# Gathered rows of five experts and of the last piece turned by transposing transfers instead of TensorE

## The chip, the cores and the metric

The kernel runs on one core of a Trainium2 chip, in one launch. The metric is the device time of an execution in microseconds (us); lower is better. The engines named below are TensorE (in rows PE, and PEld for its loads of stationary operands), VectorE (DVE), ScalarE (ACT), GpSimd (POOL) and SyncE (SP), whose queue issues most transfers.

## The reference

```python
# attention: an RWKV-5 recurrence over S = 768 steps, B = 4, H = 8, D = 48
for t in range(S):
    kt, vt, rt = k[:, :, t], v[:, :, t], r[:, :, t]
    cur = einsum('bhd,bhe->bhde', u * kt, vt)
    y[:, :, t] = einsum('bhd,bhde->bhe', rt, state + cur)
    state = w * state + einsum('bhd,bhe->bhde', kt, vt)
x = y.transpose(0, 2, 1, 3).reshape(3072, 384)
# balanced mixture of experts: 8 experts, each takes 384 tokens, by falling logit
logits = x @ w_gate
order = argsort(-logits.flatten())      # greedy: a token to its first expert with room
for e in range(8):
    mask = assigned == e
    out[mask] = relu(x[mask] @ w1[e]) @ w2[e]      # w1: 384 x 1024, w2: 1024 x 384
```

All numbers are 32-bit floats.

## The kernel before

The first 150 us or so compute the attention, the logits and the first pieces of the greedy assignment. From then on the experts run one after another, in the order in which the search on VectorE finds their tokens; expert number n below is the n-th in that order, and a last piece of 128 tokens (number 8) ends the work.

For each expert `fetch` gathers three pieces of 128 token rows of 384 floats out of DRAM into `xg` (indirect transfers on GpSimd's queue, L1518) and loads 3 MB of weights on SP's queue (L1511). The weights, `xg` and the turned rows `xT` lie in one of two pools, `self.turns[n % 2]`. The first layer contracts over the 384 features, so the rows have to be turned: `turned` (L1533) transposes each piece in three blocks of 128x128 on TensorE into a PSUM tile of `ps_t` (two buffers), and ScalarE copies each piece to `xT` (L1534).

The hidden layer is computed either directly (`hidden`, L1624; its first matmul reads all 384 rows of `xT`) or, for experts 3, 6 and 7, by a scheme of seven products (`hidden_by_seven`, L1601) that needs sums of blocks of `xT` made on VectorE (`row_sums`, L1559). The second layer: experts 1 to 5 compute two thirds of their output by seven products (`seven`, L1698) and the third piece directly (`result`, L1756). Experts 6 and 7 use fifteen products (`fifteen`, `products`, L1729).

In `seven` the products go in the order P1, P2, P5, P6, P3, P7, P4. P1, P6, P7 and P4 accumulate in one bank A, P5 and P3 in a bank B; what stands in A after P1, P6 and P7 is copied by ScalarE (L1703) before the next product adds to it, and VectorE adds the sums (L1688). Both banks are the two buffers of `ps_o`, from which `result` takes its own bank. The turn of the next expert's rows is called between P7 and P4:

```python
if name == "P4":
    between()
```

For experts 6 and 7 the turn of the next rows is called from `progress`, when the last of its due times, 1.75 (three quarters through the fifteen products), has passed. There each group of four products has a bank of `ps_o`, which ScalarE copies when the group is done (L1733).

The instructions of an engine run in the order in which they were issued. That order is chosen when the program is built: a planner takes what it holds to be ready, earlier lines of the program first, so the order can differ from the program's. `tc.issue_after(i)` keeps what is issued under it behind instruction i on that engine. The search for later experts' tokens is a chain of small VectorE instructions and a few small matmuls, spread among the products by `progress`.

Of the kernel before, what the change touches and what calls it, by code (L numbers as in the profile page):

```python
# [10 lines left out]
F32 = mybir.dt.float32  # L11
BF16 = mybir.dt.bfloat16
F16 = mybir.dt.float16
I32 = mybir.dt.int32
U8 = mybir.dt.uint8
AF = mybir.ActivationFunctionType
ALU = mybir.AluOpType
AX = mybir.AxisListType
# [1434 lines left out]
def rwkv5_eagle_then_base_layer_balanced(  # L1453
# [12 lines left out]
    nc = tc.nc  # L1466
    N, DX = out.shape
    E, _, F = moe_w1.shape
    NT = N // 128
    CAP = N // E  # L1470
# [17 lines left out]
    class Experts:  # L1488

        def __init__(self):  # L1490
            self.turns = []

        def open(self, ctx, i, **how):
            self.turns.append(ctx.enter_context(tc.tile_pool(name=f"f_turn{i}", bufs=1, **how)))

        def open_rest(self, ctx, **how):
            pool = lambda name, bufs, **kw: ctx.enter_context(tc.tile_pool(name=name, bufs=bufs, **kw))
            self.h, self.o, self.sums = pool("f_h", 2, **how), pool("f_o", 2, **how), pool("f_sums", 1, **how)
            self.first = pool("f_first", 1, **how)
            self.ps_t, self.ps_h, self.ps_o = (pool(f"f_ps_{x}", 2, space=PSUM, **how) for x in "tho")  # L1500

        def load_weights(self, n, fmax):
# [34 lines left out]
        def turn(self, ahead):  # L1537
            *_, xT = self.turned(ahead, lambda c: self.ps_t.tile([128, KD, 128], F32, name="xT_ps"))
            return xT

        def weight_sums(self, w1):
            H = F // 2
# [137 lines left out]
        def seven(self, left, right, tok, rows, at_product, between):  # L1680
            D = DX // 2
            o_sb = self.o.tile([128, NC, DX], F32, name="o_all")
            B = self.ps_o.tile([128, D], F32, name="pb_ps", tag="o_ps")
            A = self.ps_o.tile([128, D], F32, name="pa_ps", tag="o_ps")
            kept = {}

            def added(i, k, name, ps):
                nc.vector.tensor_tensor(out=o_sb[:, i, ts(k, D)], in0=kept[name], in1=ps, op=ADD)  # L1688

            for step, (name, a, b) in enumerate(self.SEVEN):  # L1690
                if name == "P2":
                    ps = self.ps_t.tile([128, D], F32, name="pc_ps", tag="xT_ps")
                else:
                    ps = B if name in ("P5", "P3") else A
                if name == "P4":
                    between()
                for j in range(KF // 2):
                    nc.tensor.matmul(ps, left[a][:, j, :], right[b][:, j, :],  # L1698
                                     start=(j == 0 and name in ("P1", "P2", "P5")), stop=(j == KF // 2 - 1),
                                     skip_group_check=True)  # L1700
                if name in ("P1", "P5", "P6", "P7"):
                    kept[name] = self.sums.tile([128, D], F32, name=f"kept_{name}")
                    nc.scalar.copy(kept[name], ps)  # L1703
                if name == "P2":
                    added(0, 0, "P1", ps)
                elif name == "P3":
                    added(0, 1, "P6", ps)
                elif name == "P7":
                    added(1, 1, "P5", kept["P7"])
                elif name == "P4":  # L1710
                    nc.scalar.copy(o_sb[:, 1, 0:D], ps)
                at_product((step + 1) / len(self.SEVEN))
            for c in range(2):
                self.leave(o_sb[:, c, :], tok[:, c:c + 1], next(rows))

        def products(self, products, out_sums, left, right, tok, rows, at_product, nk, ni):
            D = DX // nk
            count = sum(len(group) for group in products)
            own = sum(name[0] not in "po" for group in out_sums for name, _, _, _ in group)
            res = self.sums.tile([128, count + own, D], F32, name=f"res{count}")  # L1720
            o_sb = self.o.tile([128, NC, DX], F32, name="o_all")
            at = {f"o{i * nk + k}": o_sb[:, i, ts(k, D)] for i in range(ni) for k in range(nk)}
            n = 0
            for group, after in zip(products, out_sums):
                m = len(group)
                ps = self.ps_o.tile([128, m, D], F32, name="p_ps", tag="o_ps")
                for q, (name, a, b) in enumerate(group):
                    for j in range(KF // 2):
                        nc.tensor.matmul(ps[:, q, :], left[a][:, j, :], right[b][:, j, :],  # L1729
                                         start=(j == 0), stop=(j == KF // 2 - 1))  # L1730
                    at[name] = res[:, n + q, :]
                    at_product((n + q + 1) / count)
                nc.scalar.copy(res[:, n:n + m, :], ps)  # L1733
                n += m
                for name, a, op, b in after:
                    if name not in at:
                        at[name] = res[:, count + sum(k[0] not in "po" for k in at), :]
                    nc.vector.tensor_tensor(out=at[name], in0=at[a], in1=at[b], op=op)  # L1738
            for c in range(ni):
                self.leave(o_sb[:, c, :], tok[:, c:c + 1], next(rows))  # L1740
# [22 lines left out]
            self.scatter(o_sb, tok[:, c:c + 1], to)  # L1763

        FIRST_BY_SEVEN = 3, 6, 7

        def run(self, ahead, later, rows, pulls={}, xT=None):
            xT, lead = xT or self.turn(ahead), True
            row_sums = weight_sums = None
            while ahead:  # L1770
                n, _, tok, w1, w2 = ahead
                nb = tok.shape[1]
                whole = nb == NC
                many = whole and n in (E - 2, E - 1)
                sums = dict(row_sums or {}, **weight_sums) if weight_sums else None
                row_sums = weight_sums = None
                ahead = next((a for a in later if a), None)
                after = ahead and ahead[0] in self.FIRST_BY_SEVEN and ahead[2].shape[1] == NC
                late, lead = lead and not many, False
                right = (self.fifteen_w2 if many else self.seven_w2)(w2) if whole and not late else None  # L1780
                left = {}
                some = pulls.get(n, 2)
                due = [1.55, 1.75] if some == 2 else [0.75 + 1.15 * i / (some - 1) for i in range(some)]

                def half(hid):
                    nonlocal right
                    for name, (i, j) in self.BLOCKS.items():
                        left[name] = hid[:, ts(j, KF // 2), ts(i, 128)]
                    if many:
                        return  # L1790
                    last = self.sums_of(left, self.SEVEN_EARLY)
                    if late:
                        with tc.issue_after(last.ins):
                            right = self.seven_w2(w2)

                def turn():
                    nonlocal xT, row_sums
                    if ahead:
                        xT = self.turn(ahead)
                        if after:  # L1800
                            row_sums = self.row_sums(xT)

                def progress(t):
                    nonlocal weight_sums
                    if after and t > 1.1 and not weight_sums:
                        weight_sums = self.weight_sums(ahead[3])
                    while due and t > due[0]:
                        due.pop(0)
                        next(later, None)
                        if many and not due:  # L1810
                            turn()

                def at_product(part):
                    progress(1 + part)

                if sums:
                    hid = self.hidden_by_seven(sums, sums, progress)
                    half(hid)
                else:
                    hid = self.hidden(w1, xT, nb * 128, half if whole else lambda hid: None, progress, late)  # L1820
                if many:
                    self.sums_of(left, self.HID_SUMS)
                    self.fifteen(left, right, tok, rows, at_product)
                    continue
                if whole:
                    self.sums_of(left, self.SEVEN_LATE)
                    self.seven(left, right, tok, rows, at_product, turn)
                for c in range(NC - 1 if whole else 0, nb):
                    if c == nb - 1 and not whole:
                        turn()  # L1830
                    self.result(c, hid, w2, tok, next(rows))

# [186 lines left out]
```

## Time and profile before

| what | value |
|---|---|
| median of 3 runs | 394.67 us (394.22 to 394.68) |
| the profiled execution, its time | 393.36 us |
| its span | 391.6 us |
| mean granted TensorE clock, as a share of full speed | 0.995 |
| TensorE matmuls busy | 377.2 us, 96% |
| VectorE, ScalarE, GpSimd busy | 281.4, 169.3, 141.2 us |

The span runs from the first to the last instruction of one profiled execution; what lies around it is start and end. Times in rows are us from the span's start. Matmuls are pipelined, so the loads (PEld) show better than the matmuls when TensorE starts something new.

### The profile page before, as it was taken

Reading aid. Unit: us, or ns where it says so; the run is one execution under the profiler, and the core shown is the slowest. Engines: PE = TensorE matmul, PEld = TensorE weight load, DVE = VectorE, ACT = ScalarE, POOL = GpSimd, SP = SyncE. Lnnn points to the kernel's source line nnn. Section 1 sums busy time; section 2 is a strip of 40 time slices with the busy share of each in tenths; the row PEclk is TensorE's granted clock in tenths of the full one; section 3 lists DMA queues with packets and bytes.
Section 4 is the critical chain, followed back from the end, with each engine's and each line's share of the span. In section 5 each row is a group of like instructions: output and inputs, shape, how many; then the busy total and the mean of one; then the engine's idle time right before and its main releaser. Section 6 shows DMA issues by size and latency. Waiting matters only on the chain. (4 is left out here: it accounts for less than half of the span.)

```text
span 391.6 us, 9858 instructions
## 1 busy us (share of the span) xinstructions
PE 377.2 (96%) x3777; PEld 306.2 (78%) x3777; DVE 281.4 (72%) x959; ACT 169.3 (43%) x452; POOL 141.2 (36%) x173
## 2 busy tenths in 40 slices
PE   8899999999999999999999999999999999999992
PEld 7677888888877866687578899558657889989991
DVE  6755777586885788985949949888378976994530
ACT  4997989888883311312222242121222234234220
POOL 7878887767732022032122021203203212070020
PEclk9999999999999999999999999999999999999997
DMA  9999999988692164651560560109209264280010
GB/s 121 160 180 174 210 189 201 174 171 157 129 338 82 43 241 181 195 190 42 164 238 28 168 251 20 41 5 345 77 20 338 85 231 173 52 329 24 2 62 27
DMA packets 95335, 57.35 MB, mean 146 GB/s; under 512 B 77232, under 2 KB 89520, under 8 KB 95280
## 3 DMA queue, kind: packets, MB, share of 16 engines
q1 hardware_dynamic: 91936, 47.21, 48.0%
q0 software_dynamic: 3104, 9.44, 7.0%
q8 instruction: 31, 0.51, 0.6%
q14 instruction: 24, 0.20, 0.2%
q10 hardware_dynamic: 240, 0.00, 0.0%
HBM read 47.20 MB, written 9.44 MB: 145 GB/s over the span
## 5 line engine op out<-in xcount | busy, mean ns | idle before, releaser
L1624 PE MATMUL h_ps<-xT,w 128*128 128x384 f32 (+1 forms) x264 | 72.6, 427 | 0.0
L495 ACT ACTIVATE AT<-ident,dd 128x128 f32<-128x128 f32 x192 | 59.6, 392 | 2.2 <-DVE dd L448 2.1
L1624 PEld LDWEIGHTS h_ps<-xT,w 128*128 128x128 f32 x264 | 42.0, 191 | 19.6 <-issue 2.2
L1518 POOL DMA_INDIRECT xg<-x_rows,tok x22 | 22.5, 1021 | 92.4 <-PE h_ps L1624 23.7
L1750 POOL DMA_INDIRECT out_dram<-o_all,to x16 | 20.8, 1299 | 85.3 <-DVE o_all L1738 22.2
L1627 ACT ACTIVATE hid<-h_ps 128x384 f32<-128x384 f32 (+1 forms) x40 | 17.9, 449 | 54.2 <-PE h_ps L1624 50.9
L512 DVE COPY_PREDICATED AT<-mask,g_ps 64x512 f32<-64x512 uint8 (+1 forms) x48 | 32.4, 723 | 11.7 <-PE g_ps L505 9.9
L1756 PE MATMUL o_ps<-w,hid 128*128 128x384 f32 x96 | 32.5, 490 | 0.0
L505 PE MATMUL g_ps<-rT,kT 48*64 48x128 f32 (+1 forms) x768 | 26.3, 255 | 1.8 <-DVE AT L512 1.0
L436 POOL TENSOR_TENSOR kss<-krs,wk 128x384 f32<-128x384 f32 x24 | 24.3, 1016 | 8.0 <-DVE krs L340 5.0
L1756 PEld LDWEIGHTS o_ps<-w,hid 128*128 128x128 f32 x96 | 17.7, 190 | 10.6 <-issue 0.5
L545 PE MATMUL y_ps<-AT,vts 128*64 128x128 f32 x384 | 25.7, 276 | 0.0
L443 POOL TENSOR_TENSOR rk<-rk,u_bc 128x384 f32<-128x384 f32 x24 | 24.1, 1003 | 1.9
L505 PEld LDWEIGHTS g_ps<-rT,kT 48*64 48x64 f32 x768 | 20.6, 132 | 5.1 <-PE unread_ps L418 0.9
L442 POOL TENSOR_TENSOR rk<-krs 128x384 f32<-128x384 f32 x24 | 24.5, 1022 | 0.2 <-DMA krs<-in_r_dram 0.2
L545 PEld LDWEIGHTS y_ps<-AT,vts 128*64 128x64 f32 x384 | 20.6, 137 | 1.0 <-issue 0.7
L477 DVE TENSOR_TENSOR rT<-rT_ps,WR 112x512 f32<-112x512 f32 x23 | 15.7, 683 | 4.2 <-PE rT_ps L458 4.2
L448 DVE TENSOR_REDUCE dd<-rk 128x8 f32<-128x384 f32 x24 | 13.1, 545 | 6.9 <-POOL rk L443 6.9
L564 ACT COPY x<-y_ps 128x512 f32<-128x512 f32 x24 | 14.1, 586 | 5.9 <-PE y_ps L545 5.0
L458 PE MATMUL rT_ps<-ident,krs 128*112 128x128 f32 x96 | 15.4, 281 | 0.5 <-DMA krs<-in_r_dram 0.4
L1698 PE MATMUL pa_ps<-T,S 128*128 128x192 f32 x80 | 15.8, 331 | 0.0
L1729 PE MATMUL p_ps<-W,H 128*128 128x128 f32 x128 | 15.8, 275 | 0.0
(340 smaller groups left out, 834.2 us busy)
## 6 DMA issues: line engine op xcount, KB each, us to landing
w<-in_moe_w_dram SPq DMA_DIRECT2D x18, 1536.0 KB, 8.7
krs<-in_k_dram SPq DMA_DIRECT2D x24, 192.0 KB, 4.5
krs<-in_r_dram SPq DMA_DIRECT2D x24, 192.0 KB, 4.8
vts<-in_v_dram SPq DMA_DIRECT2D x24, 192.0 KB, 4.9
x_rows<-xr SPq DMA_DIRECT2D x24, 192.0 KB, 3.5
xg<-x_rows,tok POOLq DMA_INDIRECT x22, 4.0
out_dram<-o_all,to POOLq DMA_INDIRECT x16, 2.7
out_dram<-o_sb,to POOLq DMA_INDIRECT x5, 4.7
```

The lines of the kernel that those rows point to most:

```text
L436: self.nc.gpsimd.tensor_mul(self.kss[:, n % self.NS].rearrange("p (g h) d -> p g h d", g=2)[:, :, :, 0:D], src, self.wk.rearrange("p (g h) ...
L442: nc.gpsimd.tensor_mul(rk, self.krs[:, n % self.NK, 1, 0:H, 0:D], self.krs[:, n % self.NK, 0, 0:H, 0:D])
L443: nc.gpsimd.tensor_mul(rk, rk, self.u_bc)
L495: nc.scalar.mul(AT[:, z, a, :], self.ident, dd[:, h:h + 1])
L505: nc.tensor.matmul(g_ps[ts(i, PD), z, a, i * PD:], kT[rows, a, ts(i, PD)], rT[rows, a, i * PD:], start=True, stop=True)
L512: nc.vector.copy_predicated(out=AT[keys, :, :, steps], mask=mask, data=g_ps[keys, :, :, steps])
L545: nc.tensor.matmul(yv[q * PD:(q + 1) * PD, o // 2, o % 2, :], lhsT, rhs, start=(o // 2, q) not in seen, stop=stop, skip_group_check=True)
L1518: nc.gpsimd.indirect_dma_start(out=xg[:, c, :], out_offset=None, in_=x_dram[0:within, :], in_offset=bass.IndirectOffsetOnAxis(ap=tok[:, c: ...
L1624: nc.tensor.matmul(h_ps[j][:, at], w1[:, f, ts(j, 128)], xT[:, f, at], start=(f == 0), stop=(f == KD - 1))
L1627: nc.scalar.activation(hid[:, j, 0:m], h_ps[j][:, 0:m], AF.Relu)
L1750: nc.gpsimd.indirect_dma_start(out=to, out_offset=bass.IndirectOffsetOnAxis(ap=tok, axis=0), in_=o_sb, in_offset=None)
L1756: nc.tensor.matmul(o_ps, hid[:, j, ts(c, 128)], w2[:, j, :], start=(j == 0), stop=(j == KF - 1))
```

## The change

For experts 2, 3, 4, 6, 7 and the last piece (all but `BY_TENSOR = 1, 5`) the rows are turned without TensorE. Each gathered piece, 128x384 floats, is seen as 128x768 16-bit numbers. ScalarE copies it into `apart`, the 384 low halves of the floats in front of the 384 high halves. A transposing transfer on SP's queue turns the six 128x128 blocks of 16-bit numbers and writes them back over the piece in `xg`. A second ScalarE copy joins the halves again into `xT`. `apart` has two buffers. The splits and transfers (`turn_begins`) are issued after P6 and its copy, or, in experts 6 and 7, when a time of 1.3 has passed; the joins (`turn`) after P4's copy, or at the due time of before. Each split and join is queued behind the last copy of a product's bank that stands before it in the program.

```diff
@@ -13,6 +13,7 @@
 F16 = mybir.dt.float16
 I32 = mybir.dt.int32
 U8 = mybir.dt.uint8
+U16 = mybir.dt.uint16
 AF = mybir.ActivationFunctionType
 ALU = mybir.AluOpType
 AX = mybir.AxisListType
@@ -1489,6 +1490,7 @@
 
         def __init__(self):
             self.turns = []
+            self.copied = None
 
         def open(self, ctx, i, **how):
             self.turns.append(ctx.enter_context(tc.tile_pool(name=f"f_turn{i}", bufs=1, **how)))
@@ -1497,6 +1499,7 @@
             pool = lambda name, bufs, **kw: ctx.enter_context(tc.tile_pool(name=name, bufs=bufs, **kw))
             self.h, self.o, self.sums = pool("f_h", 2, **how), pool("f_o", 2, **how), pool("f_sums", 1, **how)
             self.first = pool("f_first", 1, **how)
+            self.apart = pool("f_apart", 1, **how)
             self.ps_t, self.ps_h, self.ps_o = (pool(f"f_ps_{x}", 2, space=PSUM, **how) for x in "tho")
 
         def load_weights(self, n, fmax):
@@ -1537,6 +1540,27 @@
         def turn(self, ahead):
             *_, xT = self.turned(ahead, lambda c: self.ps_t.tile([128, KD, 128], F32, name="xT_ps"))
             return xT
+
+        def turned_by_transfers(self, ahead):
+            n, xg, tok = ahead[:3]
+            xT = self.turns[n % 2].tile([128, KD, CAP], F32, name="xT")
+            nb, halves = tok.shape[1], []
+            for c in range(nb):
+                apart = self.apart.tile([128, 2, DX], U16, name="apart", bufs=2)
+                with self.behind():
+                    nc.scalar.copy(apart, xg[:, c, :].bitcast(U16).rearrange("p (f h) -> p h f", h=2))
+                turned = xg[:, c, :].bitcast(U16).rearrange("p (g t) -> p g t", t=128)
+                nc.sync.dma_start_transpose(out=turned, in_=apart.rearrange("p h f -> p (h f)"))
+                halves.append(turned)
+            yield xT
+            for c, turned in enumerate(halves):
+                with self.behind():
+                    nc.scalar.copy(xT[:, :, ts(c, 128)].bitcast(U16).rearrange("p k (t h) -> p k t h", h=2),
+                                   turned.rearrange("p (h k) t -> p k t h", h=2))
+            yield xT
+
+        def behind(self):
+            return tc.issue_after(self.copied.ins) if self.copied else ExitStack()
 
         def weight_sums(self, w1):
             H = F // 2
@@ -1693,14 +1717,16 @@
                 else:
                     ps = B if name in ("P5", "P3") else A
                 if name == "P4":
-                    between()
+                    between[1]()
                 for j in range(KF // 2):
                     nc.tensor.matmul(ps, left[a][:, j, :], right[b][:, j, :],
                                      start=(j == 0 and name in ("P1", "P2", "P5")), stop=(j == KF // 2 - 1),
                                      skip_group_check=True)
                 if name in ("P1", "P5", "P6", "P7"):
                     kept[name] = self.sums.tile([128, D], F32, name=f"kept_{name}")
-                    nc.scalar.copy(kept[name], ps)
+                    self.copied = nc.scalar.copy(kept[name], ps)
+                if name == "P6":
+                    between[0]()
                 if name == "P2":
                     added(0, 0, "P1", ps)
                 elif name == "P3":
@@ -1708,7 +1734,8 @@
                 elif name == "P7":
                     added(1, 1, "P5", kept["P7"])
                 elif name == "P4":
-                    nc.scalar.copy(o_sb[:, 1, 0:D], ps)
+                    self.copied = nc.scalar.copy(o_sb[:, 1, 0:D], ps)
+                    between[2]()
                 at_product((step + 1) / len(self.SEVEN))
             for c in range(2):
                 self.leave(o_sb[:, c, :], tok[:, c:c + 1], next(rows))
@@ -1730,7 +1757,7 @@
                                          start=(j == 0), stop=(j == KF // 2 - 1))
                     at[name] = res[:, n + q, :]
                     at_product((n + q + 1) / count)
-                nc.scalar.copy(res[:, n:n + m, :], ps)
+                self.copied = nc.scalar.copy(res[:, n:n + m, :], ps)
                 n += m
                 for name, a, op, b in after:
                     if name not in at:
@@ -1763,6 +1790,7 @@
             self.scatter(o_sb, tok[:, c:c + 1], to)
 
         FIRST_BY_SEVEN = 3, 6, 7
+        BY_TENSOR = 1, 5
 
         def run(self, ahead, later, rows, pulls={}, xT=None):
             xT, lead = xT or self.turn(ahead), True
@@ -1780,6 +1808,8 @@
                 right = (self.fifteen_w2 if many else self.seven_w2)(w2) if whole and not late else None
                 left = {}
                 some = pulls.get(n, 2)
+                none = lambda: None
+                begins = [1.3]
                 due = [1.55, 1.75] if some == 2 else [0.75 + 1.15 * i / (some - 1) for i in range(some)]
 
                 def half(hid):
@@ -1793,10 +1823,17 @@
                         with tc.issue_after(last.ins):
                             right = self.seven_w2(w2)
 
+                by_transfers = ahead and ahead[0] not in self.BY_TENSOR
+                pieces = self.turned_by_transfers(ahead) if by_transfers else None
+
+                def turn_begins():
+                    if by_transfers:
+                        next(pieces)
+
                 def turn():
                     nonlocal xT, row_sums
                     if ahead:
-                        xT = self.turn(ahead)
+                        xT = next(pieces) if by_transfers else self.turn(ahead)
                         if after:
                             row_sums = self.row_sums(xT)
 
@@ -1804,6 +1841,9 @@
                     nonlocal weight_sums
                     if after and t > 1.1 and not weight_sums:
                         weight_sums = self.weight_sums(ahead[3])
+                    if many and begins and t > begins[0]:
+                        begins.pop()
+                        turn_begins()
                     while due and t > due[0]:
                         due.pop(0)
                         next(later, None)
@@ -1824,9 +1864,11 @@
                     continue
                 if whole:
                     self.sums_of(left, self.SEVEN_LATE)
-                    self.seven(left, right, tok, rows, at_product, turn)
+                    self.seven(left, right, tok, rows, at_product,
+                               (turn_begins, none, turn) if by_transfers else (none, turn, none))
                 for c in range(NC - 1 if whole else 0, nb):
                     if c == nb - 1 and not whole:
+                        turn_begins()
                         turn()
                     self.result(c, hid, w2, tok, next(rows))
```

## Rows read from the trace of the kernel before

**Rows 1.** The page's part 1: busy us, share of the span, instructions.

```profile
PE 377.2 (96%) x3777; PEld 306.2 (78%) x3777; DVE 281.4 (72%) x959; ACT 169.3 (43%) x452; POOL 141.2 (36%) x173
```

**Rows 2.** The windows around the turns: busy us (instructions) of each engine, clock, DMA share, GB/s.

```profile
175.00:180.00 5.00, 5.00 (x36) 4.52 (x35) 4.38 (x14) 1.76 (x5) 1.00 (x1) 1.00 0.11 39
...
265.00:270.00 5.00, 4.81 (x30) 3.77 (x29) 4.96 (x17) 1.15 (x3) 0.00 (x0) 1.00 1.04 383
...
345.00:350.00 5.00, 4.40 (x30) 4.11 (x28) 5.00 (x22) 1.53 (x4) 4.70 (x2) 1.00 0.97 377
```

**Rows 3.** The tile xg: durations min/median/max in ns, first and last start; a gather's landing.

```profile
L1533 PEld LDWEIGHTS xT_ps<-ident,xg x66: 138/141/146, 150.0 to 371.2; 128*128 128x128 f32 x66
...
DMA to landing us min/median/max: 3.0/4.0/6.0
```

**Rows 4.** The timeline of turn 2: start us, length us, engine, line, operation, count.

```profile
175.38 0.32 ACT L1703 COPY kept_P<-pa_ps 128x192 f32<-128x192 f32 x1 [1.09 <-PE pa_ps L1698]
...
177.07 0.34 DVE L1688 TENSOR_TENSOR o_all<-kept_P,pb_ps 128x192 f32<-128x192 f32 x1
...
177.28 0.63 PEld L1698 LDWEIGHTS pa_ps<-T,S 128*128 128x128 f32 x4
...
177.88 0.74 PEld L1533 LDWEIGHTS xT_ps<-ident,xg 128*128 128x128 f32 x6
...
178.24 0.32 ACT L1703 COPY kept_P<-pa_ps 128x192 f32<-128x192 f32 x1 [2.54 <-PE pa_ps L1698]
...
178.61 0.30 PEld L1698 LDWEIGHTS pa_ps<-T,hid 128*128 128x128 f32 x2
...
179.16 0.31 PEld L1533 LDWEIGHTS xT_ps<-ident,xg 128*128 128x128 f32 x3 [0.25 <-ACT xT L1534]
...
180.52 4.82 PEld L1756 LDWEIGHTS o_ps<-w,hid 128*128 128x128 f32 x16
...
185.85 0.95 PEld L1624 LDWEIGHTS h_ps<-xT,w 128*128 128x128 f32 x4
```

**Rows 5.** The timeline of turns 3 and 6.

```profile
209.75 0.63 PEld L1698 LDWEIGHTS pa_ps<-T,S 128*128 128x128 f32 x4
...
211.18 0.30 PEld L1698 LDWEIGHTS pa_ps<-T,hid 128*128 128x128 f32 x2
...
212.77 0.35 PEld L1756 LDWEIGHTS o_ps<-w,hid 128*128 128x128 f32 x2
...
308.31 0.30 PEld L1698 LDWEIGHTS pa_ps<-T,hid 128*128 128x128 f32 x2
...
308.48 0.35 DVE L1688 TENSOR_TENSOR o_all<-kept_P,pb_ps 128x192 f32<-128x192 f32 x1
...
309.95 4.87 PEld L1756 LDWEIGHTS o_ps<-w,hid 128*128 128x128 f32 x16
```

**Rows 6.** The timeline of expert 5's gather and turn.

```profile
273.49 0.98 POOL L1518 DMA_INDIRECT xg<-x_rows,tok  x1 [0.30 <-issue]
...
276.61 0.31 PEld L1533 LDWEIGHTS xT_ps<-ident,xg 128*128 128x128 f32 x3 [0.55 <-ACT xT L1534]
```

**Rows 7.** The timeline of turn 7, in expert 6's fifteen products.

```profile
333.97 0.59 ACT L1733 COPY res<-p_ps 128x512 f32<-128x512 f32 x1 [2.94 <-PE p_ps L1729]
...
339.32 1.00 SPq L1511 DMA_DIRECT2D w<-in_moe_w_dram  x2
...
344.88 0.62 PEld L1601 LDWEIGHTS h_ps<-xT,w 128*128 128x128 f32 x4
```

**Rows 8.** DMA issues: size of one, median us from issue to landing.

```profile
w<-in_moe_w_dram SPq DMA_DIRECT2D x18, 1536.0 KB, 8.7
...
krs<-in_k_dram SPq DMA_DIRECT2D x24, 192.0 KB, 4.5
...
out_dram<-o_all,to POOLq DMA_INDIRECT x16, 2.7
...
wp<-in_w_dram SPq DMA_DIRECT2D x2, 0.4 KB, 2.0
```

## The prediction

> **What bounds the kernel now.** I read the page's busy times first: TensorE's matmuls hold 96% of the span [rows 1]. Then the windows around the places that the change touches: TensorE is busy for all or nearly all of the 5 us, at the full granted clock, so nothing is to be had from the clock; VectorE holds 4.4 to 5.0 us of 5, ScalarE 1.8 at most [rows 2]. So TensorE bounds, with VectorE close behind it. Next the transposes: 66 of them from 150 us on, six loads in 0.74 us, so each holds the array 0.12 us [rows 3, 4]. The change takes 48 of the 66 away: 48 x 0.12 = 5.8 us, 1.5% of the span, is about the most it can give. I call the turning of expert n's rows turn n; turns 2, 3, 4 and 6 stand in the seven products of the expert before, turn 7 and that of the last piece (turn 8) in the fifteen.
>
> **What the removal gives, turn by turn.** A turn's worth is not its transposes but how much earlier the next work starts. In turn 2 the loads of P7 end at 177.91 (177.28 + 0.63) and the result's loads begin at 180.52. Four loads take 0.63, so P4's eight want 1.30, and a small matmul of the search between them 0.16: 2.61 - 1.46 = 1.15 us would be saved [rows 4]. But P4 adds into the bank that P7's copy on ScalarE reads, 178.24 to 178.56, and begins at 178.61. The first six transposes fill just that wait. Without them it lies open, unless other matmuls are put there; then P4 ends at 179.91 and, with the small matmul, 0.45 us is saved. What could fill it is the result's first matmuls, which need bank B, read last by VectorE's sum of P3 from 177.07 to 177.41: free in time. In the trace P4's first loads stand ahead of the turn's last transposes, against the program's order, so the planner does put ready work into holes; I take the hole of turn 2 as filled. Turn 3 likewise: P7 ends at 210.38, 212.77 - 210.38 - 1.30 = 1.09 filled, 212.77 - 211.18 - 1.30 = 0.29 open. In turn 6 VectorE reads B only at 308.48, after P4 has begun, so the hole stays: 309.95 - 308.31 - 1.30 = 0.34, or some 1.1 if it could be filled [rows 5].
>
> Turn 4 would give up to 1.1 too, but what is late next is expert 5, still turned by TensorE: its third gather is issued at 273.49 and its last transposes run at 276.61, 3.1 us later, where a gather takes 3.0 us at least and 4.0 at the median [rows 3, 6]. That gather waits for a list out of VectorE's chain, and VectorE is busy 4.96 of 5 us at 265 to 270 [rows 2]. TensorE would come sooner and wait: 0. Turn 7's nine transposes are worth 9 x 0.12 = 1.1, but behind them, at 345 to 350, VectorE is busy all 5.0 us and TensorE only 4.40 [rows 2], so VectorE sets the pace there: I take 0. Turn 8 comes after that, 3 x 0.11 = 0.33, kept whole.
>
> Sum: 1.15 + 1.09 + 0 + 0.34 + 0 + 0.33 = 2.9 us. With every hole open: 0.45 + 0.29 + 0.34 + 0.33 = 1.4. With all filled and everything passed on: 1.15 + 1.09 + 1.1 + 1.1 + 1.1 + 0.33 = 5.9.
>
> **What is added on ScalarE.** Sixteen pieces, two copies of 128x768 16-bit numbers each. A copy of 192 columns takes 0.32 and one of 512 takes 0.59 [rows 4, 7]: 0.83 ns for a column and 0.16 fixed, so 0.80 for 768, an estimate (from above 0.96, twice the 0.48 that the same line gives 384 columns; from below nothing speaks for less). That is 32 x 0.80 = 25.6 us for 16 x 0.48 = 7.7 removed, on an engine with 3 us of 5 free: hidden as such. What matters is who stands behind a split in ScalarE's order: P7's copy, on which P4 waits.
>
> **What is added on the queue.** Sixteen transfers of 192 KB, SBUF to SBUF, on SP's queue, transposing. No row shows one. From below, the smallest transfer, 0.4 KB, lands 2.0 us after its issue; from above, the 192 KB loads of the crowded first stage take 4.5. The nearest are the scatters of 128 rows, 192 KB too, 2.7, since they run where the transfer engines are as idle as here (busy share 0.11 around turn 2) [rows 2, 8]. I take X = 2.7 and keep 2.0 to 4.5, and more, since transposing may cost what a copy doesn't.
>
> **The chain that must stay hidden.** The halves have two buffers, so the third split waits for the first transfer. In turn 2, from the end of P6's copy (175.38 + 0.32 = 175.70): split 0.8, transfer X, third split 0.8, transfer X, join 0.8. It ends at 178.1 + 2X, 183.5 with 2.7. The next hidden layer reads all three pieces in its first matmul; it began at 185.85 and would begin at 184.7 [rows 4]. So 1.2 us to spare: the whole gain up to X = 3.3, none at 3.9, and beyond that every 0.1 us of X costs 0.2 in each seven. Turn 7 starts behind the first group's copy, 333.97 + 0.59 = 334.56, and ends at 334.56 + 2.4 + 5.4 = 342.4, against 344.88 [rows 7]. Turn 8, one piece, has more to spare. The first two splits end at 177.3, before P7's copy is due at 178.24: no delay, if the third isn't queued ahead of it.
>
> SP's queue carries the weights too: 1.5 MB twice, 8.7 us each to landing [rows 8]. In the sevens the transfer engines are idle; in turn 7 the last piece's weights are issued at 339.32, just behind where the third transfer would be, 334.56 + 0.8 + 2.7 + 0.8 = 338.9 [rows 7]. They aren't wanted before expert 7 is done, so behind the transfers they lose nothing.
>
> The Trainium skill has a rule against the change ("VectorE: DVE Perf Modes", section Rules for kernel authors): transpose a block of 128x128 on TensorE if PSUM will do as the destination. Its section The three transpose paths gives a 16-bit block 390 ns on TensorE and 1309 ns through the crossbar of the transfer engines; were the six blocks of a piece taken in turn, X would be an estimated 7.9 us by that and each seven 8 us late. Another page ("DMA: Bandwidth & Descriptors", Latency and other measured facts) measured transposing transfers at 261 GB/s, an estimated 0.75 us for 192 KB, by which X is about 2.75 and the sum stays. No run so far shows either.
>
> **Rivals.** (a) *Late transfers.* X lies with the loads, not with the scatters. At 4.5 the chain of a seven ends at 187.1, 1.25 us behind the old start, four times; turn 7 is 1.1 late; less 0.33: 5.8 us slower, 400.5; at 4.2 +2.8, 397.5; at 5, 405. It decides from X = 3.9. For it: no row transposes; against it: idle transfer engines. (b) *Blocks one after other*: if each of a piece's six blocks paid the 2.0 us of the smallest transfer, X = 12: 178.1 + 24 is 16 us late in each seven, about the same in turn 7, some 80 us slower, 475; at 1 us a block X = 6, each seven 4.3 late, turn 7 4.1, 415. This is where the skill's figure per block would lead. (c) *ScalarE blocked.* The third split is queued ahead of P7's copy; that copy starts at 175.70 + 0.8 + 2.7 + 0.8 = 180.0 instead of 178.24, P4's loads run from 180.4 to 181.7, the result starts 1.2 us late (0.6 with a hole partly filled), four times, less 0.33: 2 to 4.5 slower, 398. For it: the program's order; against it: the planner passes over what isn't ready. (d) *Weights first* in turn 7: 3 MB lie ahead of the third transfer, 8.7 us or more, and the join ends near 351, 6 late: net +3, 398. (e) *No difference*: X about 3.6, or the holes open and a little of (c): within 0.8 us.
>
> **How the numbers follow.** The profiled execution took 393.36, 1.8 around its span of 391.6; the median of the runs is 1.3 above it, 394.67. The sum is one of differences, so it comes off the median: 394.67 - 2.9 = 391.8. Chances: hidden 0.51, its own range 388.8 (all 5.9) to 393.3 (1.4); (a) 0.13; (b) 0.07; (c) 0.10; (d) 0.06; (e) 0.13. Some 0.2%, 0.8 us, is what a measurement of this kernel can tell from no change. Faster is the first case, 0.51; same is (e) and the mildest of (a), 0.14; slower the rest, 0.35. The range runs from 389.0 to 402, with (c), (d), (e) and most of (a) inside; (b) and the worst of (a), some 0.12, are left out.
>
> **What would show it.** Right: the transfers land about 2.7 us after issue; ScalarE's copies of 768 take 0.8; the result's first matmuls stand between P7 and P4 in turns 2 and 3; no hidden layer waits for a join; TensorE waits more before expert 5's transposes and around 348. Wrong: a first hidden matmul that waits for ScalarE's join (a, b, d), or P7's copy later behind P7's last load than the 0.33 us of now (178.24 - 177.91) (c). The first thing to fail would be X, the one term without a row of its own.

## The result, and the profile after

The changed kernel takes 396.39 us in the median of its runs (394.38 to 396.91), beside 394.68 for the kernel before in the same session (394.08 to 395.24): a ratio of 1.0033, 95% interval 1.0021 to 1.0044, so 0.33% slower, where 391.8 and faster were forecast. The profiled execution took 396.48, with a span of 394.7.

The page first: its parts 1, 2 (the line of the clock) and 6. Against [rows 1] TensorE has lost 1.4 us of work and its share is a point lower; one slice has a lower clock; the transfers land 2.8 us after issue in the median.

```profile
PE 375.8 (95%) x3729; PEld 303.6 (77%) x3729; DVE 280.8 (71%) x959; ACT 188.4 (48%) x468; POOL 140.4 (36%) x173
...
PEclk9999999999999999999999899999999999999998
...
xg<-apart SPq DMA_TRANSPOSE x16, 2.8
```

A page of sums can't say where 3.1 us of span went (1.7 by the medians, since the execution profiled before lies 1.3 below its median). So I cut both timelines at the first weight load of each hidden layer and of what follows it. "Rows behind" and "rows behind, 6 by TensorE" are experiments told below.

| stretch, us | before | after | rows behind | and 6 by TensorE |
|---|---|---|---|---|
| start to hidden 1 | 152.38 | 153.28 | 152.68 | 151.95 |
| hidden 1 to 2 (turn 2) | 33.47 | 32.32 | 32.33 | 32.32 |
| hidden 2 to 3 (turn 3) | 32.74 | 31.20 | 31.73 | 31.73 |
| hidden layer 3 | 14.85 | 19.49 | 14.95 | 14.94 |
| its sevens, to hidden 4 (turn 4) | 16.35 | 15.62 | 15.62 | 15.62 |
| hidden 4 to 5 | 33.34 | 33.58 | 33.56 | 33.43 |
| hidden 5 to 6 (turn 6) | 32.17 | 31.43 | 31.87 | 32.17 |
| hidden layer 6 | 14.74 | 17.37 | 16.31 | 14.73 |
| its fifteens, to hidden 7 (turn 7) | 14.84 | 13.69 | 13.69 | 13.69 |
| hidden 7 to 8 (turn 8) | 29.08 | 28.67 | 28.27 | 28.83 |
| hidden 8 to the end | 17.64 | 18.05 | 18.09 | 17.69 |

The first stretch is unchanged code; over all the kernels run here it varies from 151.95 to 153.93. The last row uses spans given to 0.1. Behind the first stretch, every turn by transfers is shorter than before. What outweighs them is two hidden layers: 4.64 us in the third and 2.63 in the sixth.

Turn 2 goes as forecast. Its timeline after, answering to [rows 4] and 0.90 later: the splits, the transfers, the result's first two loads in the hole between P7 and P4, P4 with its eight loads in one piece, the last join, the hidden layer.

```profile
176.50 1.57 ACT L1551 COPY apart<-xg 128x768 uint16<-128x768 uint16 x2
...
177.36 5.04 SPq L1553 DMA_TRANSPOSE xg<-apart  x3
...
178.78 0.35 PEld L1783 LDWEIGHTS o_ps<-w,hid 128*128 128x128 f32 x2
...
179.51 1.27 PEld L1722 LDWEIGHTS pa_ps<-T,hid 128*128 128x128 f32 x8 [0.38 <-ACT kept_P L1727]
...
183.95 0.92 ACT L1558 COPY xT<-xg 128x768 uint16<-128x768 uint16 x1 [0.27 <-DMA xg<-apart]
...
185.60 0.30 PEld L1648 LDWEIGHTS h_ps<-xT,w 128*128 128x128 f32 x2
```

Turn 3 is where it breaks. Two rows of the kernel before stood not ahead of the prediction: VectorE's first row sum of expert 3 (L1559, L1583 after), and the first of two small matmuls in which TensorE takes the search's answer (L1079, L1080 after).

```profile
213.26 0.62 DVE L1559 TENSOR_TENSOR first_S<-xT 128x192 f32<-128x192 f32 x2
...
218.51 0.17 PE L1079 MATMUL st_ps<-acc,ones 128*128 128x24 bf16 x1
```

After, in the timeline of the same place (a bracket is the idle time of that engine before the row, and what ended it):

```profile
212.44 0.83 ACT L1551 COPY apart<-xg 128x768 uint16<-128x768 uint16 x1 [1.65 <-DMA xg<-apart]
...
215.59 0.92 ACT L1558 COPY xT<-xg 128x768 uint16<-128x768 uint16 x1 [1.28 <-DMA xg<-apart]
...
216.72 0.92 ACT L1558 COPY xT<-xg 128x768 uint16<-128x768 uint16 x1 [0.21 <-DMA xg<-apart]
...
217.67 0.63 DVE L1583 TENSOR_TENSOR first_S<-xT 128x192 f32<-128x192 f32 x2 [2.86 <-ACT xT L1558]
...
219.02 0.28 DVE L1061 TENSOR_SCALAR full_e<-counts 128x128 f32<-128x128 f32 x1
...
220.64 0.24 DVE L1076 SCALAR_TENSOR_TENSOR acc<-em,fmax,past 128x24 bf16<-128x24 f32 x1
...
220.93 0.17 PE L1080 MATMUL st_ps<-acc,ones 128*128 128x24 bf16 x1 [2.35 <-DVE acc L1076]
...
220.94 0.10 PEld L1081 LDWEIGHTS <-rest_of 128*128 128x128 bf16 x1 [2.58 <-issue]
...
221.59 1.30 PEld L1625 LDWEIGHTS hb_ps<-xT,w 128*128 128x128 f32 x4
...
222.87 1.30 PEld L1625 LDWEIGHTS hb_ps<-first_S,first_T 128*128 128x128 f32 x4
...
224.15 1.06 PEld L1625 LDWEIGHTS h_ps<-first_S,first_T 128*128 128x128 f32 x4
```

Read it from below. Four loads at 221.59 take 1.30 us where four take 0.63 to 0.68 elsewhere. Ahead of them TensorE stood for 2.58 us at its search matmul, in the middle of a hidden layer whose operands were all there. The matmul waits for `acc` of VectorE's search. The search stands in VectorE's order behind the row sums, and those waited 2.86 us for the last join, which now ends at 217.64. The windows over that place show the clock (columns as in [rows 2]):

```profile
218.00:221.00 3.00, 0.65 (x7) 0.42 (x5) 2.90 (x19) 0.49 (x2) 1.13 (x1) 1.00 0.18 66
221.00:222.00 1.00, 1.00 (x7) 1.00 (x7) 1.00 (x11) 0.00 (x0) 0.00 (x0) 0.75 0.00 0
222.00:224.00 2.00, 2.00 (x8) 2.00 (x7) 1.80 (x12) 0.52 (x1) 0.00 (x0) 0.50 0.56 78
224.00:226.00 2.00, 2.00 (x11) 1.86 (x9) 1.85 (x4) 0.93 (x2) 0.00 (x0) 0.77 1.04 382
```

TensorE is idle for most of three microseconds at the full clock, and then runs at the lower of its two levels, 1.2 GHz, from 221.5 to about 224.9 (worked out from the means 0.75 and 0.77). The three groups of loads there cost 0.62, 0.62 and 0.38 more than 0.68: some 1.6 us on top of the stall.

### The profile page after: what moved, and what is told of

Same layout as the page of the kernel before. It is cut to its first block, busy times and chain, and to the rows that moved or that the text cites. A ratio compares the mean times of both kernels' runs of the same rounds, so it can differ in the third digit from the quotient of the medians.

```text
span 394.7 us, 9805 instructions
## 1 busy us (share of the span) xinstructions
PE 375.8 (95%) x3729; PEld 303.6 (77%) x3729; DVE 280.8 (71%) x959; ACT 188.4 (48%) x468; POOL 140.4 (36%) x173
## 4 chain that ended last, share of the span: by engine, by line
PE 56%; issue 16%; DVE 9%; DMA 7%; ACT 5%; POOL 5%; POOLq 0%; another core or an unknown queue 0%; DVEq 0%; ACTq 0%
PE h_ps L1648 12%; PE y_ps L546 5%; PE g_ps L506 4%; PE pa_ps L1722 4%; PE h_ps L1625 3%; DMA xg<-apart 3%; PE hb_ps L1625 3%; DMA xg<-x_rows,tok 3%; PE e_h_ps L1891 3%; PE o_ps L1783 3%; ACT AT L496 2%; PE kT_ps L459 2%; PE kv_ps L525 2%; PE pb_ps L1722 2%; PE x_ps L596 2%
## 5 line engine op out<-in xcount | busy, mean ns | idle before, releaser
L1777 POOL DMA_INDIRECT out_dram<-o_all,to x16 | 19.0, 1186 | 89.6 <-DVE o_all L1765 44.8
L1613 ACT ACTIVATE hid<-kept_P 128x384 f32<-128x384 f32 x18 | 9.4, 523 | 19.9 <-DVE kept_P L1617 17.9
L1558 ACT COPY xT<-xg 128x768 uint16<-128x768 uint16 x16 | 14.4, 919 | 3.9 <-DMA xg<-apart 3.7
```

## The experiments

I had two theories after the result. **V:** VectorE's row sums wait, in order, for the last join; the search and TensorE's search matmuls stand behind them; the clock falls on top. **W:** the transfers and the added copies cost time in themselves, by load on the queues or on ScalarE. Each kernel is timed beside the kernel before, and the ratios are to it.

**Three buffers for the halves.**

```diff
-                apart = self.apart.tile([128, 2, DX], U16, name="apart", bufs=2)
+                apart = self.apart.tile([128, 2, DX], U16, name="apart", bufs=3)
...
-            o_sb = self.o.tile([128, DX], F32, name="o_sb")
+            o_sb = self.o.tile([128, DX], F32, name="o_sb", bufs=1)
```

> The changed kernel with three buffers for the halves, so that the third split needn't wait for the first transfer (the result's o_sb gets one buffer for two, to make room). Theory V (VectorE waits in order for the last join of turn 3, the search chain and TensorE's small search matmuls stand behind it, the clock falls): the joins of turn 3 end about 2 us sooner, VectorE's wait of 2.86 us goes to under 1, TensorE's 2.58 us wait and the stretch at half clock go; 396.4 - 2.6 - 1.5 = 392 to 393.5. Theory W (the sixteen transfers and thirty-two copies cost in themselves, wherever they stand): unchanged, 396 to 396.8.

Measured: 397.83, ratio 1.0065 (1.0044 to 1.0087). My number missed, and the timeline says why: the third transfer went out at 212.06 instead of 213.30, and landed later, at 217.26; after, the last join could begin at 216.72.

```profile
212.06 1.67 SPq L1553 DMA_TRANSPOSE xg<-apart  x1
...
216.81 1.73 ACT L1558 COPY xT<-xg 128x768 uint16<-128x768 uint16 x2 [2.50 <-DMA xg<-apart]
...
218.58 0.63 DVE L1583 TENSOR_TENSOR first_S<-xT 128x192 f32<-128x192 f32 x2 [3.11 <-ACT xT L1558]
...
221.84 0.17 PE L1080 MATMUL st_ps<-acc,ones 128*128 128x24 bf16 x1 [2.82 <-DVE acc L1076]
```

The tile of the halves in the window of that transfer alone:

```profile
DMA to landing us min/median/max: 5.2/5.2/5.2
```

Three transfers issued within 2.7 us are all landed 7.9 us after the first issue (209.39 to 217.26). The third took 5.2 us, where after it took 3.4 (issued at 213.30): issued earlier beside the others, it landed no earlier, so a buffer doesn't bring the last join forward. The join ended at 218.54, 0.9 later than after, in a run whose hidden layer 1 already stood 0.65 later. The edit didn't move the suspected cause, so it doesn't decide between V and W.

**The row sums behind the search's answer.** The same transfers and joins; only the sums are issued behind the instruction that asks for the next weights, the end of the search.

```diff
-            nc.vector.tensor_scalar(out=number, in0=fmax[0:1, :], scalar1=1.0, scalar2=float(E),
+            self.asked = nc.vector.tensor_scalar(out=number, in0=fmax[0:1, :], scalar1=1.0, scalar2=float(E),
...
-                        if after:
-                            row_sums = self.row_sums(xT)
...
+                if weight_sums:
+                    here = any(i is self.asked.ins for i in nc.cur_bb.bb.instructions)
+                    with tc.issue_after(self.asked.ins) if here else ExitStack():
+                        sums = dict(self.row_sums(xT), **weight_sums)
```

> The changed kernel with VectorE's row sums queued behind the search chain's last step before the next weights are asked for; transfers and copies as they are. Theory V: the chain no longer stands behind the joins, so VectorE waits for no join in turn 3, hidden layer 3 takes 15 to 16 us for 19.5, full clock; 392 to 393.5. Theory W: unchanged, 396 to 396.8.

Measured: 391.13, ratio 0.9913 (0.9901 to 0.9926). The timeline of turn 3:

```profile
216.16 0.92 ACT L1558 COPY xT<-xg 128x768 uint16<-128x768 uint16 x1 [0.17 <-DMA xg<-apart]
...
216.66 0.17 PE L1080 MATMUL st_ps<-acc,ones 128*128 128x24 bf16 x1
...
216.74 0.62 PEld L1625 LDWEIGHTS h_ps<-xT,w 128*128 128x128 f32 x4
...
217.11 0.36 DVE L1583 TENSOR_TENSOR first_S<-xT 128x192 f32<-128x192 f32 x1 [0.17 <-ACT xT L1558]
```

The last join ends at 217.08, only half a microsecond sooner than after, in a run whose hidden layer 1 stood 0.60 sooner, and still behind the hidden layer's first load. Now the search's matmul stands ahead of that load without a wait, as it did before, and the layer takes 14.95 us at a granted clock of 1.00 throughout. All transfers and copies are still there: W falls as an explanation of the loss. The time is below V's number, 392 to 393.5.

**The rows of experts 3, 6 and 7 on TensorE,** those that have row sums.

```diff
-        BY_TENSOR = 1, 5
+        BY_TENSOR = 1, 3, 5, 6, 7
```

> Transfers only for turns 2, 4 and 8, where no row sums follow; turns 3, 6 and 7 by TensorE again. Theory V: nothing on VectorE waits for a join; the gains of turns 2 (1.15) and 8 (0.33) are kept, turn 4 gives 0 to 0.7: 392.5 to 393.4. Theory W: seven of sixteen pieces, so +0.4 x 1.7 us: 395.2 to 395.7.

Measured: 392.38, ratio 0.9948 (0.9934 to 0.9962): 0.12 below V's number and 2.8 below W's.

**Only expert 3's rows by transfers.**

```diff
-        BY_TENSOR = 1, 5
+        BY_TENSOR = 1, 2, 4, 5, 6, 7, 8
```

> Transfers only for turn 3, all others by TensorE. Theory V: the whole loss of hidden layer 3 (4.6 us with the clock's fall, 2.6 without) less turn 3's gain of 1.1 to 1.5: 396 to 398, slower than before although only three of sixteen pieces are left. Theory W: three of sixteen of +1.7: 395.0, not to be told from before.

Measured: 399.26, ratio 1.0129 (1.0111 to 1.0147). One turn by transfers instead of six, and the slowest kernel of all; 1.3 above V's 396 to 398. In its timeline the first two transfers of this turn land 5.0 and 4.6 us after issue:

```profile
218.75 0.91 ACT L1558 COPY xT<-xg 128x768 uint16<-128x768 uint16 x1 [1.63 <-DMA xg<-apart]
...
219.70 0.63 DVE L1583 TENSOR_TENSOR first_S<-xT 128x192 f32<-128x192 f32 x2 [4.25 <-ACT xT L1558]
...
222.96 0.18 PE L1080 MATMUL st_ps<-acc,ones 128*128 128x24 bf16 x1 [3.75 <-DVE acc L1076]
```

Three kernels now agree. From the end of the last join to the search's matmul it is 3.29 us after (217.64 to 220.93), 3.30 with three buffers (218.54 to 221.84) and 3.30 here (219.66 to 222.96): the row sums and the search, in order, on VectorE. TensorE's wait grows with the join, 2.35, 2.82, 3.75, and hidden layer 3 with it: 19.49, 19.81, 20.78. What stands behind the join on VectorE sets the loss, not the number of transfers.

**The kernel before, with its row sums behind the answer too** (the second edit on the kernel before).

> The kernel before, all rows turned by TensorE, with only the row sums moved behind the search's answer on VectorE. If the transfers' late joins are what the row sums wait for, there is no such wait here to remove (their two first additions stand at 213.26 without a wait): 394.4 us, within 0.6 of the kernel before, and hidden layer 3 stays at about 14.9 us. If instead the move is a gain of its own (five additions of 0.35 us taken out from ahead of the search three times), it gives much of the 3.3 us here too: 391 to 393.

Measured: 393.64 beside 393.53, ratio 1.0005 (0.9996 to 1.0013). So the move is no gain of its own. The 3.3 us of the second experiment are what the transfers give once nothing ahead of the search waits for their joins.

**Row sums behind, and expert 6's rows on TensorE.** After, TensorE stood 1.11 us in hidden layer 6 too, for a search matmul at 318.61 behind the row sums (316.22 to 317.65); moving the sums took 1.06 off that layer. In the second experiment it was still 1.57 us longer than before, though no row sum waits there. The weights of expert 7 land later: VectorE's first sum of them (L1548, L1572 after) stands 11.21 us behind their issue before, 13.94 after and 13.32 in the second experiment.

```diff
-        BY_TENSOR = 1, 5
+        BY_TENSOR = 1, 5, 6
```

> The changed kernel with the row sums behind the search's answer, and expert 6's rows turned by TensorE again. If turn 6 by transfers costs hidden layer 6 its 1.6 us (16.3 against 14.7), because the weights of expert 7 land later after their issue (13.3 us against 11.2) when the next gathers are issued only 3.8 us behind them instead of 7.6, then that layer is back at 14.7 and turn 6's own gain of some 0.4 is lost: 391.1 - 1.6 + 0.4 = 389.9, from 389.5 to 390.5. If the layer is long because everything ahead of it came 3 us sooner, or because the row sums were moved, it stays long: 391.1 to 391.8.

Measured: 389.36, ratio 0.9899 (0.9885 to 0.9913). That is 0.14 below the range; but the kernel before took 393.53 beside it and 394.39 beside the second experiment, from which the range was reckoned, and the gain on the kernel before, 4.2, lies within the 3.9 to 4.9 that the range amounts to. The timeline around it, the weights' issue, the next gathers, and the sum that reads the weights:

```profile
312.32 1.06 SPq L1514 DMA_DIRECT2D w<-in_moe_w_dram  x2
...
319.89 0.99 POOL L1521 DMA_INDIRECT xg<-x_rows,tok  x1 [5.84 <-PE hb_ps L1625]
...
323.50 0.69 DVE L1572 TENSOR_TENSOR first_T<-w 128x512 f32<-128x512 f32 x1 [3.22 <-DMA w<-in_moe_w_dram]
```

The sum comes 11.18 us behind the issue, the gathers 7.57 behind it (before 11.21 and 7.58; after 13.94 and 4.92; in the second experiment 13.32 and 3.81), and the layer takes 14.73 us. From the first hidden layer to the end the two traces differ by 1.27 us (236.42 and 235.15); their ratios to the kernel before overlap. That turn 6 by transfers is what makes that layer long is shown; that it does so by gathers which share the transfer engines with the weights fits these four traces and the other five (13.92 with the gathers 4.77 behind in the run with three buffers, 11.1 to 11.4 with 7.57 behind in the rest), but no run moved the gathers alone.

**And expert 4's rows on TensorE as well.**

```diff
-        BY_TENSOR = 1, 5, 6
+        BY_TENSOR = 1, 4, 5, 6
```

> As the run before, with expert 4's rows on TensorE too. If turn 4 is worth nothing, because expert 5's gathered rows are what is late next, it lies within 0.3 us of the run before. If the transfers of turn 4 were worth their 1.1 us of transposes, it is about 1 us slower; if they hold up expert 5's list or rows, 0.3 to 0.5 us faster.

Measured: 389.89, ratio 0.9904 (0.9889 to 0.9918): 0.53 slower than the run before it in the median, between the 0.3 of the first case and the 1 of the second, with intervals that overlap. From hidden layer 1 to the end its trace is 0.5 longer too. Whether turn 4 is worth nothing or 0.5 us, four runs of each can't tell.

## Why the prediction was wrong

**The step that failed** is "The chain that must stay hidden": it compared the end of the last join with the next hidden layer's first matmul, and took that for the joined rows' only reader. The row sums of experts 3, 6 and 7 read them too, and they stand on VectorE ahead of the search, which stands ahead of TensorE's search matmuls. The rows of busy time [rows 1, 2] had made VectorE "close behind", but it was never asked which of its instructions reads `xT`, and when. In the trace of before that is the row at 213.26, 5.3 us ahead of hidden layer 3 at 218.59. The deadline in turn 3 was therefore not the hidden layer but TensorE's arrival at the search matmul, about 218.4 after, less the 3.3 us of sums and search: 215.1. Even with X at 2.7 the join would have ended at 207.92 + 2.4 + 5.4 = 215.7, an estimate by the prediction's own sum, 0.6 late; with the 3.7 and 3.4 that the first and third transfer of this turn took it ended at 217.64.

**X.** The median is 2.8, where 2.7 was taken, but it rests on the three landings that the trace holds, 3.68, 2.74 and 2.77; the others are read from the copies that waited for them. No hidden layer of the changed kernel waits for a join: rivals (a) and (b) fell. But X is not one number: the third transfer of turn 6 had 2.7 and the one of turn 8 2.8, the second of turn 4 3.7, and in turn 3 the first had 3.7 (208.68 to 212.44), the second 5.6 (210.02 to 215.59). Of the two pages weighed there, the Trainium skill's "DMA: Bandwidth & Descriptors", Latency and other measured facts, has 261 GB/s, which with the 2.0 us of the smallest transfer gave an estimated 2.75; the transfers with 2.74 and 2.77 agree with that sum. The rate itself no run shows: with two transfers of turn 3 under way a window below has 157 GB/s. Six blocks at the price for one in the Trainium skill's "VectorE: DVE Perf Modes", The three transpose paths, an estimated 7.9, are not what a whole piece costs here.

**ScalarE.** Estimated 0.80; the split takes 0.83 and the join 0.92. P7's copy in turn 2 starts 0.33 us behind P7's last load (179.14 and 178.81), as before: rival (c) didn't occur. Neither did (d): the weights of turn 7 are issued at 345.54, behind the third transfer.

**The sum.** Cleared of the failed step, the second experiment's column shows its terms. Turn 2: 1.14, forecast 1.15. Turn 3: 1.01, forecast 1.09, in which a small search matmul of 0.16 such as the one counted in turn 2 was left out (the 1.54 of after contains the search matmuls, which slid behind the hidden layer's first loads). Turn 6: 0.30, forecast 0.34. The holes were filled where I had taken them as filled. Turn 4: 0.73, of which 0.2 is given back at once; by the trace of the last experiment it is worth some 0.5, which the times don't tell from the forecast of 0. Turn 7 was mis-sized: 1.15 instead of 0, and nothing of it is given back between hidden 7 and 8, so a VectorE that is busy all the time in [rows 2] did not set the pace there. Turn 8 was 0.33 on paper; the last two rows of the table together gain 0.0 after, 0.36 and 0.20 in the two experiments. From hidden layer 1 on the second experiment is 2.8 us shorter than before, against 2.9 forecast; that this agrees so well is partly luck, since turn 7's gain and hidden layer 6's loss, both unforeseen, nearly cancel. For that loss, 1.57 us, no term stood in the sum.

**The clock** had a part I had excluded ("nothing is to be had from the clock"). Of the twenty runs of the changed kernel fourteen were granted a mean clock of 0.991 to 0.993 and took 395.76 to 396.91; six were granted 0.996 or 0.997 and took 394.38 to 394.87. In the profiled execution the windows from 221 to 226 lose 0.25, 1.00 and 0.46 us of the full clock, together 0.4% of the span, about the distance between the two groups; in no other stretch of 20 us from 150 to 390 is the clock below 1.00. So the fall behind the stall is worth about 1.9 us where it happens, as much as the whole measured loss. That the other thirteen runs fell at the same place is inferred from their clocks, not seen.

Open: hidden layer 8, 0.4 us longer in two of the four traces of the table, was not followed up, nor why the transfers of turn 3 took longer than those of the other turns, up to 5.6 us after and 5.0 and 4.6 for the first two where they were the only ones.

## What to carry to other kernels

When a result comes later than it did, list every reader of it on every engine, and for each what stands behind it in that engine's order; the deadline is that of the earliest such chain, not that of the reader you optimise for. Much of a transfer's gain can be had by moving the reader: here five additions issued behind a search turned 0.3% slower into 0.9% faster (1.0% with one turn given back to TensorE, which the runs don't tell apart). Where the granted clock falls behind a stall, as it did here, the stall costs more than its length (2.58 us and some 1.6 more), so price it by both.

## What the runs showed of the hardware

Transposing transfers kept the transfer engines busy about twice as long for a byte as a load of weights did. Two windows of the changed kernel: in the first two transfers of turn 3 and a scatter of results are under way, in the second a load of weights; the last two columns are the transfer engines' busy share and GB/s.

```profile
210.00:212.00 2.00, 2.00 (x13) 1.64 (x12) 1.97 (x6) 0.32 (x1) 0.92 (x1) 1.00 0.91 157
...
226.00:228.00 2.00, 2.00 (x17) 1.86 (x17) 0.91 (x3) 0.83 (x3) 0.00 (x0) 1.00 1.07 393
```

The engines are 0.91 busy at 157 GB/s, where the weights move at 393 with a share of 1.07. The page counts 12,801 packets more than before for 3.2 MB more, some 250 bytes each. So the "idle transfer engines" of the prediction, 0.11 around turn 2 in [rows 2], were not idle once the transfers ran, and a third one in flight is not free.

The clock: a wait of TensorE of 2.58 us in hidden layer 3 was followed by 1.2 GHz from 221.5 to about 224.9; waits of 3.05 us with three buffers and 3.98 with turn 3 alone were followed by it too (granted clock 0.50 from 224 to 226 in both). Waits of 1.1 and 1.36 us in hidden layer 6 left it at 1.00.
